# A planned order kept word for word for its first 520 entries and ordered anew behind them: gated linear attention followed by a spatial gating block

## The chip, the core and the metric

The kernel runs on one core of one Trainium2 chip. The metric is the device time of one launch in microseconds (us). Engines are named as the profile names them: PE (TensorE matmuls) and PEld (its weight loads), DVE (VectorE), ACT (ScalarE), POOL (GpSimd) and SP (SyncE, which issues nearly all DMAs here).

## What is computed

A recurrence with a 48x48 state for each of 4 x 8 heads runs over 768 steps; its output, heads side by side, goes through a gated MLP with a mixing over the sequence.

```python
def _attn_ref(q, k, v, alpha):            # each (4, 8, 768, 48)
    for t in range(S):
        state = alpha[:, :, t, :, None] * state + einsum('bhd,bhe->bhde', k[:, :, t], v[:, :, t])
        y[:, :, t] = einsum('bhd,bhde->bhe', q[:, :, t], state)
    ...
def _moe_ref(x, w_in, w_spatial, b_spatial, w_out):   # x: (4, 768, 384)
    h = np.maximum(x @ w_in, 0.0)
    u, v = (h[..., :d_ff // 2].copy(), h[..., d_ff // 2:].copy())
    v_n = (v - mu) / np.sqrt(var + 1e-06)
    v_s = np.einsum('ts,bsd->btd', w_spatial, v_n) + b_spatial[None, :, None]
    return ((u * v_s) @ w_out).astype(np.float32)
```

## The kernel before

Each batch's 768 steps are cut into 6 chunks of 128; chunks are numbered 0 to 23 over the four batches. For a chunk the kernel loads `alpha`, `k`, `q`, `v` (four DMAs of 192 KB, L883, on SP), takes the logarithm of alpha (`lns`, ACT), sums it on PE (`cums`, L898 to L901), takes the exponential with both signs on ACT (`einvs`, L908, and `eexps`, L910) and of the chunk's total (`ebc`, L915), multiplies k and q by them (`kts` on POOL or DVE, `qts` on DVE), transposes both on PE (`trk`, L988, two chunks at once) and evicts them (`evs`). PE then forms the update of the state (`upd`, L932), DVE adds the old state (`z`, L393), POOL or DVE scales it (`S`) and one engine casts it (`sb`). PE also forms the scores (`sc`, L944), DVE masks them (`ms`, L949), and PE makes the chunk's output (`y`, L960 and L416), which ACT or DVE evicts into `xT` (`xe`).

For each batch the MLP follows: `v` (L1005, three matmuls of 512 columns for each of 6 sequence tiles) with ReLU eviction `ve`, statistics `bn` (DVE), `rs` (ACT), `nm` (DVE) and normalization `vn`; `u` (three matmuls of 384 columns for each of 4 feature tiles and 2 halves of the sequence) with eviction `ue`; the mixing `s` (six matmuls of 384 columns, in a part of four and a part of two), to which DVE adds the bias (`se`, L1152); the product `g` of both (POOL or DVE, L189); the output projection `o` (four matmuls), eviction `oe` and store `st` (SP, L1184).

No scheduler orders this. Each of these steps is an `Op` with a number, given in the order in which the functions create them. The string `PLAN` is the order in which they are emitted, and `replay` emits them so: a letter for the engine (P PE, D DVE, A ACT, G POOL, S SP), the number of the step, and behind `@` the PSUM banks that it takes. Every engine works through its own entries in the order of the table; across engines only semaphores hold it back. There are eight banks of PSUM; an entry may take a bank when all users of the bank's last holder stand ahead of it in the table, and on the chip PE then waits for the last of them.

```python
for word in plan.split():
    ...
    for slot, n in zip(op.take, banks):
        assert held[n] is None or all(u.done for u in held[n].users), op.key
        held[n] = slot
        slot.bank = n
    op.emit(eng)
```

Steps whose numbers are used below (b is the batch, th the half of the sequence, d the feature tile):

| entry | step |
|---|---|
| P745, D746 | update matmuls of chunk 18; scaling of its state |
| A747, A779, A851, A792, A790 | cast of that state; `eexps` 20; `lns` 23; `ebc` 21; `einvs` 21 |
| G781, G793 | `kts` of chunks 20 and 21 |
| G671, G675, G679, G683 | `g` of b 2, th 0, d 0, 1, 2, 3 |
| P700, P703, P706 | output projection of b 2, tiles 0, 1, 2 |
| P593, A594, P604, P723, P596 | `v` of b 2 tile 2 and its eviction; `v` of tile 3; `cums` 18; `u` of b 2, d 0, th 0 |
| D899, D915, D922, G907, G911, G919 | `g` of b 3: (d 1, th 0), (d 1, th 1), (d 3, th 1); (d 3, th 0), (d 0, th 1), (d 2, th 1) |

Of the kernel before, what the change touches and what calls it, by code (L numbers as in the profile page):

```python
# [63 lines left out]
P436@4 A437 A441 A385 D264 D439 P272@0 D367 D267 D428 D431 D386 P521@1 P372@4 A514 A273 P565@6 P376@2 A377 A432 A552  # L64
P442@7 A568 P529@0 D443 D522 P456@3 D433 D434 A435 A566 A567 D373 P452@7 P553@1 P518@2,5 A519 A554 A556 D520 A555 P457
D458 D530 D570 G569 G523 G557 G459 P444@4 P445 P448@5 D446 P453 D454 P468@6 P449 D558 D450 P533@7,4 P524@2,0 P572@1,3
D525 G451 G455 P472@5 P469 P460@2 P473 D526 D534 D535 G531 G447 D474 S623 A559 P575@7 D576 A573 P461 S625 S612 S563
A615 D470 D462 P616@4 P527@5 P536@1 A627 S613 A574 P579@7,3 P588@6,0 G577 A617 A528 D589 A618 A537 P628@5 A629 A571
G475 P538@2 A630 P464@1 S624 S614 S730 S718 S721 S626 S720 G620 D621 D581 D580 S733 S732 P476@6 G631 G578 P541@3
P584@7 A539 A619 A542 P465 S784 S719 A477 D632 P634@5,4 D590 A636 D466 D585 S731 A722 P591@3 S786 S772 S785 S773 S835  # L70
S774 A592 S787 S775 G622 G532 P582@1 A583 D635 D540 P637@7 P482@6 A633 A483 P723@5 G586 G471 D638 G639 A724 P645@3,4
P640@0,2 D543 G463 G587 P479@7 P604@6 P596@1 D646 D642 D641 A734 A726 D647 G729 G467 A605 A741 G727 P593@3 P600@6 A594
P735@0 D606 D595 A738 D480 P648@4 P643@3 A544 D545 D546 D597 A649 P488@2 A644 A788 A601 A489 D547 P653@4 P660@7 P745@6
A654 D746 D655 A736 A607 D608 D610 P491@3 P664@4 A661 A665 A737 P650@6 A492 A776 G739 P598@1 D651 D609 P485@4 D652
A486 A725 D747 P666@7 A667 D740 P602@6 P662@4 P789@3 A656 A603 P676@7 P672@0 P753@6 A599 A790 A791 P777@1 A778 A792
A779 S484 S847 S836 S837 A839 A783 S838 S848 A663 S849 D657 D658 D659 D754 D728 P677 P673 P680@6 P688@5 D674 P681
P668@0 D794 D755 D678 D782 G781 G795 D682 P799@7 P669 G793 D800 P689 G675 D690 D670 P742@6,4 P796@7,3 A851 A780 D797
P696@5 A743 A798 G683 G679 P808@0 P697 P852@7 P840@6 A841 A842 A853 A843 A854 D744 P748@3,4 P757@1,2 D698 G801 G671
D749 D809 D758 P692@5 P693 D694 D750 P684@3 P703@0 P685 P700@5 G846 D759 A701 D686 P706@4 D856 D845 D707 A704 P760@5
A761 P751@0 A752 A802 P803@6,7 D805 G844 G855 P812@3,2 P858@4,5 G810 G687 G699 G691 A859 G695 D813 P762@0 S850 P861@7  # L80
P765@3 D814 D804 P712@2 P815@6 A756 A763 P806@0 A860 D862 D764 D857 A816 A807 A766 P864@5,7 P869@4,1 S702 P715@6 D866
D871 D767 D870 D865 P828@7 A829 D830 P824@1 P820@3 P817@7 A821 A768 A818 A825 G863 P872@4 A873 S705 A716 S481 S259
S268 S487 S265 S493 S490 S271 S708 S262 S478 S274 G811 P867@5 D819 P826@3 P822@1 D868 P877@4 D769 D771 A827 S717 A831
A823 A878 A770 A713 D832 P874@3 D833 D834 P890@5 P888@1 P884@4 D879 D875 D876 A880 D881 D882 P916@6 P709@2 A710 P896@3
P886@7 P900@0 A887 A889 A885 A891 P892@2 D883 P897 D898 G899 P893 P901 P908@5 P909 D894 D902 P904@2 P905 G903 P917
P912@0 P913 P920@3 D906 D895 D918 G919 D907 P929@6 P923@2 P921 S711 A930 S931 A924 S925 S714 D914 D910 D911 P926@6
G915 D922 P932@2 A933 D927 S928 S934 P938@3 D939 S940 P935@6 A936 S937 P941@3 D942 S943
"""


# [1174 lines left out]
```

## Time and profile before

| | |
|---|---|
| timed runs | 138.52, 138.55, 138.70 us, median 138.55 |
| span of the profiled execution | 137.9 us (137.862), 5298 instructions |
| matmul records and weight loads | 2108 and 2122 |
| bytes over DMA | 28.66 MB, 76521 packets, 63056 of them under 512 B |
| granted PE clock | 1.000 |

The profiled execution's own time outside its span is not listed; the timed median is 0.69 us above the span. In the profile a line such as "75.14 0.33 PE L932 ..." gives the start, the length, the engine, the source line, the tiles and the number of merged instructions. Lengths of matmuls are modelled and overlap the next one: a 384-column matmul is listed at 0.327 us, while four in a row start 0.16 us apart.

### The profile page before, as it was taken

What the parts mean: (1) busy time and instruction counts of PE and PEld (TensorE: products, weight loads), DVE (VectorE), ACT (ScalarE), POOL (GpSimd) and SP (SyncE); (2) the same over time, 40 slices, a digit from 0 to 9 for tenths busy, and PEclk for the clock granted to TensorE, in tenths of its full rate; (3) what the DMA queues carried; (4) which work ended last, traced back from release to release, by engine and by line L of the source; (5) the groups of instructions that cost most, each with busy time, mean ns of one, the idle gap of its engine ahead of it and who ended that gap; (6) DMA issues with size and microseconds to landing.
All of it is one profiled execution on the core that took longest, in us unless ns stands there. A gap on an engine that the chain in (4) does not pass through costs nothing.

```text
span 137.9 us, 5298 instructions
## 1 busy us (share of the span) xinstructions
PE 130.1 (94%) x2108; PEld 79.4 (58%) x2122; DVE 120.2 (87%) x300; ACT 107.7 (78%) x261; POOL 86.6 (63%) x146
## 2 busy tenths in 40 slices
PE   6999998999999999799999999999999999999990
PEld 3365555565566556466657676656576765566560
DVE  6259999989989999899899999997999999974960
ACT  3476998999999799699997989999865796953040
POOL 7355899993499799761079989520799841004550
PEclk9999999999999999999999999999999999999999
DMA  3999999499989788699999898999960597101064
GB/s 88 370 372 381 344 349 361 106 373 382 355 162 281 159 168 165 124 186 188 193 204 201 164 209 156 189 186 216 213 134 5 187 349 270 63 0 57 0 233 172
DMA packets 76521, 28.66 MB, mean 208 GB/s; under 512 B 63056, under 2 KB 74960, under 8 KB 76496
## 3 DMA queue, kind: packets, MB, share of 16 engines
q1 hardware_dynamic: 76464, 28.32, 77.8%
q8 instruction: 16, 0.26, 0.8%
q14 instruction: 9, 0.07, 0.2%
q0 software_dynamic: 32, 0.00, 0.0%
HBM read 23.60 MB, written 4.72 MB: 205 GB/s over the span
## 4 chain that ended last, share of the span: by engine, by line
PE 60%; DMA 19%; POOL 8%; issue 3%; SPq 3%; ACT 3%; DVE 0%; POOLq 0%; ACTq 0%
PE bank L1005 43%; DMA raw_w<-in_moe_w_spatial_dram 6%; DMA kc<-in_k_dram 5%; DMA raw_w<-in_moe_w_out_dram 4%; DMA ac<-in_alpha_dram 4%; PE bank L960 3%; SPq L883 3%; PE bank L944 2%; PE bank L988 2%; PE bank L416 2%; POOL w_row L180 2%; POOL kt L189 2%; PE bank L932 1%; PE bank L898 1%; POOL state L189 1%
## 5 line engine op out<-in xcount | busy, mean ns | idle before, releaser
L1005 PE MATMUL bank<-w_spT,vn 128*128 128x384 bf16 x192 | 35.6, 327 | 0.0
L189 POOL TENSOR_TENSOR gT<-vs,uT 128x384 bf16<-128x384 f32 x28 | 25.7, 933 | 14.1 <-DVE vs L1152 14.1
L189 POOL TENSOR_TENSOR kt<-kc,binv 128x384 bf16<-128x384 f32 x22 | 20.2, 928 | 22.3 <-ACT binv L908 15.2
L1005 PEld LDWEIGHTS <-vn 128*128 128x128 bf16 x192 | 17.5, 98 | 11.2 <-issue 0.3
L1005 PE MATMUL bank<-w_in,xT 128*128 128x512 bf16 x58 | 17.4, 380 | 1.6 <-ACT xT L178 0.7
L1005 PE MATMUL bank<-xT,w_in 128*128 128x384 bf16 x96 | 18.7, 326 | 0.0
L1005 PE MATMUL bank<-w_out_sb,gT 128*128 128x384 bf16 (+1 forms) x100 | 18.4, 320 | 0.0
L1152 DVE TENSOR_TENSOR vs<-bank,bsp_bc 128x384 f32<-128x384 f32 x31 | 16.3, 549 | 2.4 <-PE bank L1005 2.3
L949 DVE TENSOR_TENSOR ptm<-bank,mask 128x512 bf16<-128x512 f32 x28 | 17.9, 682 | 0.5 <-PE bank L944 0.3
L178 ACT COPY kqT<-bank 128x512 bf16<-128x512 bf16 (+1 forms) x20 | 15.0, 793 | 3.1 <-PE bank L988 1.9
L1067 DVE BATCH_NORM_STATS2 stats<-v_sb 128x6 f32<-128x512 bf16 x24 | 16.4, 683 | 0.6 <-ACT v_sb L184 0.5
L184 ACT ACTIVATE v_sb<-bank 128x512 bf16<-128x512 f32 x20 | 11.7, 597 | 2.0 <-PE bank L1005 1.7
L184 ACT ACTIVATE uT<-bank 128x384 bf16<-128x384 f32 x27 | 12.4, 494 | 0.7 <-PE bank L1005 0.6
L1005 PEld LDWEIGHTS <-w_in 128*128 128x128 bf16 x96 | 9.0, 97 | 6.7 <-DVE ptm L949 0.3
L189 DVE TENSOR_TENSOR qt<-qc,bank 128x384 bf16<-128x384 f32 x24 | 12.6, 545 | 0.2 <-DMA qc<-in_q_dram 0.2
L1005 PEld LDWEIGHTS <-gT 128*128 128x128 bf16 x100 | 9.2, 98 | 5.8
L178 ACT CAST xT<-bank 128x384 bf16<-128x384 f32 x23 | 10.4, 482 | 1.1 <-PE bank L416 0.8
L843 DVE TENSOR_TENSOR ptm<-bank,mask 128x512 bf16<-128x512 f32 x16 | 10.3, 683 | 0.2 <-PE bank L836 0.2
L242 PE MATMUL bank<-junk 128*128 128x512 f32 (+3 forms) x14 | 8.8, 763 | 1.0 <-DVE junk L1231 1.0
L1005 PEld LDWEIGHTS <-xT 128*128 128x128 bf16 x72 | 6.2, 97 | 6.2 <-ACT xT L178 1.2
L178 ACT COPY raw_w<-bank 128x384 f32<-128x384 f32 x8 | 3.8, 479 | 7.3 <-PE bank L1005 7.2
L393 DVE TENSOR_TENSOR zs<-bank,state 128x384 f32<-128x384 f32 x16 | 8.8, 548 | 0.5 <-PE bank L932 0.4
(162 smaller groups left out, 264.3 us busy)
## 6 DMA issues: line engine op xcount, KB each, us to landing
ac<-in_alpha_dram SPq DMA_DIRECT2D x14, 192.0 KB, 4.4
kc<-in_k_dram SPq DMA_DIRECT2D x14, 192.0 KB, 4.4
qc<-in_q_dram SPq DMA_DIRECT2D x14, 192.0 KB, 4.4
vc<-in_v_dram SPq DMA_DIRECT2D x14, 192.0 KB, 4.2
raw_w<-in_moe_w_spatial_dram SPq DMA_DIRECT2D x3, 768.0 KB, 7.8
out_dram<-raw_w SPq DMA_DIRECT2D x11, 192.0 KB, 2.1
out_dram<-o_sb SPq DMA_DIRECT2D x9, 192.0 KB, 2.0
ac<-in_alpha_dram SPq DMA_DIRECT2D x2, 768.0 KB, 6.7
```

The costliest lines, as they stand in the source:

```text
L178: nc.scalar.copy(out=out, in_=in_)
L184: nc.scalar.activation(out=out, in_=in_, func=AF.Relu)
L189: ENG[eng].tensor_tensor(out=out, in0=in0, in1=in1, op=ALU.mult)
L242: nc.tensor.matmul(out=banks[n][:, 0:cols].rearrange("p (a b) -> p a b", a=4), lhsT=junk, rhs=junk[:, None, 0:cols // 4].to_broadcast([128 ...
L393: lambda _: nc.vector.tensor_tensor(out=zs[i % 3], in0=tp(), in1=state[(i - 1) % 3], op=ALU.add),
L843: nc.vector.tensor_tensor(out=ptm[n2][:, ci, s], in0=banks[sl.bank].rearrange("p (hp t) -> p hp t", hp=HP), in1=mask[:, 3][:, None, :].to_ ...
L883: nc.sync.dma_start(out=t[x].rearrange("p hp s d -> p (hp s) d"), in_=src[b, :, c * C:c * C + C, :].rearrange("h s d -> s h d"))
L949: nc.vector.tensor_tensor(out=ptm[n2][:, ci, s], in0=banks[sl_p[s].bank].rearrange("p (hp t) -> p hp t", hp=HP), in1=mask[:, 2][:, None, : ...
L960: nc.tensor.matmul(out=place(to, 3 * hp + (0, 1, 1, 2)[x]), lhsT=heads(vb, hp, x), rhs=ptm[n2][:, ci, x // 2, hp, :], start=(turn == 0), s ...
L1005: nc.tensor.matmul(out=ps, lhsT=lhsT, rhs=rhs, start=first and n == 0, stop=last and n == len(pairs) - 1)
L1067: nc.vector.bn_stats(out=stats[tt % 2], in_=v_sb[n2][:, tt, :])
L1152: nc.vector.tensor_tensor(out=vs[d], in0=banks[sl.bank][:, 0:TH], in1=bsp_bc[:, th, :], op=ALU.add)
```

## The change

Only `PLAN` changes. Its first 520 entries are the same word for word. The other 424 are the same steps in a new order, with other banks, and for 38 of them another engine: 14 go from ACT to DVE and 14 from DVE to ACT, 4 from DVE to POOL, 3 from ACT to POOL, 2 from POOL to DVE and 1 from POOL to ACT. PE keeps its 124 entries, and no instruction's shape changes. The plan before reaches its 521st entry at about 75.3 us on PE; on SP the first changed entry is the load at 66.0 us. Two of the lines on each side:

```diff
-P668@0 D794 D755 D678 D782 G781 G795 D682 P799@7 P669 G793 D800 P689 G675 D690 D670 P742@6,4 P796@7,3 A851 A780 D797
...
-A761 P751@0 A752 A802 P803@6,7 D805 G844 G855 P812@3,2 P858@4,5 G810 G687 G699 G691 A859 G695 D813 P762@0 S850 P861@7
...
+D754 A747 P680@6 P673 A779 A851 A792 A790 D674 P669 P681 P688@2 D728 D782 D670 G781 S775 S785 G793 S786 A791 G675 D682
...
+S787 G795 S848 G683 D794 P689 S490 S835 P742@0,1 D743 A744 P676@7 P677 D678 G679 D690 P696@5 G671 P757@0,1 D758
```

Three places show what moves. First POOL, around the key scalings of chunks 20 and 21 (`kt_102` from `binv_106` and `binv_107`) and the four products `gT_142` of batch 2, th 0. Before:

```order
L189 TENSOR_TENSOR kt_102<-kc,binv_106 128x8x48
L180 CAST vb_113<-vc 128x8x48
L189 TENSOR_TENSOR kt_102<-kc,binv_107 128x8x48
L189 TENSOR_TENSOR gT_142<-vs_153,uT_137 128x384
L189 TENSOR_TENSOR gT_142<-vs_155,uT_137 128x384
L189 TENSOR_TENSOR gT_142<-vs_154,uT_137 128x384
L189 TENSOR_TENSOR state_128<-zs_125,bc_119 128x384
L189 TENSOR_TENSOR gT_142<-vs_152,uT_137 128x384
```

The same place on POOL in the changed kernel:

```order
L189 TENSOR_TENSOR kt_102<-kc,binv_106 128x8x48
L189 TENSOR_TENSOR kt_102<-kc,binv_107 128x8x48
L189 TENSOR_TENSOR gT_142<-vs_153,uT_137 128x384
L180 CAST vb_113<-vc 128x8x48
L189 TENSOR_TENSOR gT_142<-vs_155,uT_137 128x384
L189 TENSOR_TENSOR gT_142<-vs_154,uT_137 128x384
L189 TENSOR_TENSOR gT_142<-vs_152,uT_137 128x384
L189 TENSOR_TENSOR state_127<-zs_124,bc_118 128x384
```

The cast `vb_113` now stands behind the first product, and the last product stands ahead of a state update. Second ACT, where the evictions of `v` (`v_sb_138`) and `u` (`uT_137`) of batch 2 begin; `bank_64` to `bank_71` are PSUM banks 0 to 7. Before:

```order
L184 ACTIVATE v_sb_138<-bank_70 128x512
L178 CAST vb_112<-vc 128x8x48
L184 ACTIVATE v_sb_138<-bank_67 128x512
L915 ACTIVATE bc_118<-bank_64 64x4 x2
L1077 ACTIVATE rstd_146<-mvs_144,eps_tile 128x2
```

ACT in the changed kernel, from the eviction A594 on:

```order
L184 ACTIVATE v_sb_138<-bank_70 128x512
L184 ACTIVATE v_sb_138<-bank_69 128x512
L184 ACTIVATE uT_137<-bank_71 128x384
L908 ACTIVATE binv_108<-bank_64 128x384
L184 ACTIVATE uT_137<-bank_70 128x384
L888 ACTIVATE la_100<-ac 128x8x48
```

Bank 6 (`bank_70`) goes from `v` of tile 2 to `u` of d 0 within four ACT instructions. Third DVE at the end of the program, with the additions `vs` and the products `gT_143` of batch 3. Before:

```order
L189 TENSOR_TENSOR gT_143<-vs_152,uT_135 128x384
L1152 TENSOR_TENSOR vs_154<-bank_70,bsp_bc 128x384
L189 TENSOR_TENSOR gT_143<-vs_155,uT_135 128x384
L1152 TENSOR_TENSOR vs_153<-bank_64,bsp_bc 128x384
L1152 TENSOR_TENSOR vs_152<-bank_69,bsp_bc 128x384
L189 TENSOR_TENSOR gT_143<-vs_152,uT_135 128x384
L189 TENSOR_TENSOR gT_143<-bank_67,uT_135 128x384
L180 COPY o_sb_156<-bank_70 128x384
```

DVE at the same place in the changed kernel:

```order
L1152 TENSOR_TENSOR vs_152<-bank_68,bsp_bc 128x384
L1152 TENSOR_TENSOR vs_153<-bank_69,bsp_bc 128x384
L186 TENSOR_SCALAR uT_135<-bank_71 128x384
L189 TENSOR_TENSOR gT_143<-vs_153,uT_135 128x384
L189 TENSOR_TENSOR gT_143<-bank_70,uT_135 128x384
L1152 TENSOR_TENSOR vs_153<-bank_64,bsp_bc 128x384
L189 TENSOR_TENSOR gT_143<-vs_153,uT_135 128x384
```

The product of d 3 (from a bank directly) now stands ahead of the last addition instead of last, two products have changed sides with POOL, and the copy of an output tile has gone to ACT.

More of the change, by code (lines that the diff above doesn't have):

```diff
@@ L66 @@
 D458 D530 D570 G569 G523 G557 G459 P444@4 P445 P448@5 D446 P453 D454 P468@6 P449 D558 D450 P533@7,4 P524@2,0 P572@1,3
[L67 to L75, printed above, removed]
@@ L76 @@
-A779 S484 S847 S836 S837 A839 A783 S838 S848 A663 S849 D657 D658 D659 D754 D728 P677 P673 P680@6 P688@5 D674 P681
-P668@0 D794 D755 D678 D782 G781 G795 D682 P799@7 P669 G793 D800 P689 G675 D690 D670 P742@6,4 P796@7,3 A851 A780 D797
-P696@5 A743 A798 G683 G679 P808@0 P697 P852@7 P840@6 A841 A842 A853 A843 A854 D744 P748@3,4 P757@1,2 D698 G801 G671
-D749 D809 D758 P692@5 P693 D694 D750 P684@3 P703@0 P685 P700@5 G846 D759 A701 D686 P706@4 D856 D845 D707 A704 P760@5
-A761 P751@0 A752 A802 P803@6,7 D805 G844 G855 P812@3,2 P858@4,5 G810 G687 G699 G691 A859 G695 D813 P762@0 S850 P861@7
@@ L81 @@
[L81 to L85, printed above, removed]
@@ L86 @@
-P912@0 P913 P920@3 D906 D895 D918 G919 D907 P929@6 P923@2 P921 S711 A930 S931 A924 S925 S714 D914 D910 D911 P926@6
-G915 D922 P932@2 A933 D927 S928 S934 P938@3 D939 S940 P935@6 A936 S937 P941@3 D942 S943
+D525 G451 G455 P472@5 P469 P460@2 P473 D526 D534 D535 G531 A615 P464@7 S612 S623 S563 D470 D474 A571 A627 G447 A559
+P575@6 G532 A573 D576 P616@4 P461 A574 S730 A734 A619 G475 D462 P465 P628@6 P527@5 A528 G577 G578 D466 P536@3 A537
+P579@2,1 D581 P588@5,7 D589 D590 P584@0 A629 A617 A630 G620 A618 P541@3 A542 S626 S625 D632 S624 S613 D621 P538@1
@@ new lines @@
+P479@5 A539 A480 S614 S784 D580 D585 G631 S259 A622 S718 P482@3 A483 G586 G587 P735@4 P634@5,1 A635 A738 S847 S772
+D543 D636 P591@2 P582@0 A583 A788 P637@3 P476@6 A477 D638 D540 P640@1,5 D642 P645@3,0 D647 A592 D646 A544 D641 P602@7
+P593@6 A722 A594 P604@5 A605 A603 S733 P723@0 P596@6 A724 A597 A776 G467 P598@3 S721 A599 A725 A726 G463 G471 P488@7
+D595 D606 S719 A607 G633 G639 G729 G727 P643@1 D644 P648@6 A736 A737 P789@5 A649 D545 D547 D489 P600@3 A601 A546 S773
+S731 D608 P491@1 D492 P650@2 P777@7 S268 P664@1 A665 P653@3 A654 P660@6 P662@1 P485@3 D610 A778 A663 D651 D609 D741
@@ new lines @@
+A780 D652 A661 D655 A656 S732 S774 S720 D740 D486 D657 D659 D658 G739 P666@2 P672@1 A667 P668@4 P753@2 P745@3 D746
+D754 A747 P680@6 P673 A779 A851 A792 A790 D674 P669 P681 P688@2 D728 D782 D670 G781 S775 S785 G793 S786 A791 G675 D682
+S787 G795 S848 G683 D794 P689 S490 S835 P742@0,1 D743 A744 P676@7 P677 D678 G679 D690 P696@5 G671 P757@0,1 D758
+P748@7,6 P796@4,3 D783 G755 G756 P697 P852@0 P684@2 D750 P685 P808@6 S265 S849 S837 D749 D759 A797 D686 A839 P840@4
+A798 A853 A843 A854 P700@7 P799@3 P692@1 S836 S838 D800 D698 D701 G855 A841 G801 A842 D856 D845 G844 P706@2 A707 P693
@@ new lines @@
+D694 P703@5 A704 S705 P751@0 P760@2 P812@4,7 A752 A761 G846 G802 D809 G810 D813 D814 P803@1,5 P858@0,3 A860 A859
+P762@2 P861@4 P765@7 A763 P815@3 A816 S262 S850 S702 D805 S478 S493 D804 P806@1 D766 A807 D862 P869@0,5 D871 P864@2,7
+P828@3 P817@5 A829 S271 S481 A818 P826@1 P824@3 G863 G691 G811 D865 D866 P867@5 A857 D870 P872@0 D819 A868 A827 D830
+D767 D764 A873 A831 D832 A825 D834 P820@7 P874@5 A821 P884@0 A875 G695 G699 P877@1 P822@7 G687 P715@5 P712@3 A768 D769
+D833 D770 D876 P890@2 A771 P908@4 A878 D879 A880 A716 D885 D881 D713 S714 S274 S717 P916@1 P900@6 P904@0 P892@5 A883
@@ L88 @@
+D882 P917 P893 P901 D894 D902 G903 S487 P905 P888@3 P896@5 P909 D918 D906 P709@6 P897 P886@1 P912@0 A710 S711 A887
+A889 A891 P920@6 G895 P921 S708 S484 D910 D898 P913 D823 D899 G907 P929@2 P923@3 A930 S931 D922 D914 A924 S925 P926@0
+A927 S928 D915 G919 G911 P932@2 A933 S934 P938@3 D939 S940 P935@0 A936 S937 P941@2 D942 S943
 """
```

## The prediction, on record before the run

> **What bounds the kernel now.** I read the page's busy shares first, then the table of stretches from the change to the last matmul and behind it, and then the chain that ended last.
>
> ```profile
> PE 130.1 (94%) x2108; PEld 79.4 (58%) x2122; DVE 120.2 (87%) x300; ACT 107.7 (78%) x261; POOL 86.6 (63%) x146
> 75.40:134.40 59.00, 58.43 (x841) 36.61 (x844) 53.18 (x121) 43.49 (x109) 32.68 (x56) 1.00 0.62 155
> 134.40:137.90 3.50, 0.00 (x0) 0.00 (x0) 0.31 (x1) 0.10 (x1) 0.00 (x0) 1.00 0.48 171
> 129.33 5.01 PE bank L1005 x34
> 134.35 0.36 DVE raw_w L180
> ```
>
> The columns of the stretches are length, then PE, PEld, DVE, ACT and POOL busy, granted clock and DMA share. In the 59.0 us that the change can touch, PE is idle for 59.00 - 58.43 = 0.57 us. DVE is busy 53.18 us of them (90%), ACT 74%, POOL 55%. The chain's last rows are 34 matmuls, then one copy at 134.35; behind 134.4 the last store and the end of the program take 3.5 us, which the change leaves as they are, since both tables end with the same four steps. **So PE is the bound, it is nearly full, and its work does not change.** An order can only remove waits of PE or add them.
>
> **How much waiting is there to remove.** 0.57 us is the upper end from the idle column. It is not exact: 14 matmul records are missing (2122 loads, 2108 matmuls), and a missing one shows as idle. On the other side modelled ends cover waits:
>
> ```profile
> 96.46 3.09 PE L1005 MATMUL bank<-w_spT,vn 128*128 128x384 bf16 x18
> 99.59 0.33 PE L932 MATMUL bank<-vb,kt 128*128 128x96 bf16 x4
> 101.54 0.82 PE L1005 MATMUL bank<-w_spT,vn 128*128 128x384 bf16 x4
> 102.20 0.33 PE L932 MATMUL bank<-vb,kt 128*128 128x96 bf16 x4
> ```
>
> Four matmuls of 384 columns take 102.20 - 101.54 = 0.66 us to the next start, 0.163 each. Eighteen should take 2.93 us; they took 99.59 - 96.46 = 3.13. The 0.20 us is a wait of PE for the state update of chunk 20 that the idle column hardly shows. The other waits that I find by this pitch are small ones, under 0.1 us each, some 0.25 together. I take **0.45 us as the headroom**, with 0.57 as its end.
>
> **Changes of tile shape.** A step of 32, 48 or 64 rows or columns costs PE something at its borders:
>
> ```profile
> 68.29 0.57 PE bank L988 x32
> 100.57 1.04 PE bank L988 x64
> ```
>
> One transposing step takes 0.57 us, two in a row 1.04, so that the second adds 0.47 and a border costs about 0.09. The new order parts these two transposing steps, but puts other small steps together instead. Counted over both tables from entry 521 on, full tiles change to a smaller shape 9 times and back 9 times in each, and the output steps meet score or transposing steps 4 times in each. This term is 0.
>
> **Engines.** A moved eviction changes the load of its engine:
>
> ```profile
> L189 POOL TENSOR_TENSOR gT<-vs,uT 128x384 bf16<-128x384 f32 x17 | 15.4, 926 | 14.1 <-DVE vs L1152 14.1
> 86.00:96.00 10.00, 9.61 (x28) 1.00 0.98 200
> ```
>
> 14 steps each way between ACT and DVE leave both about where they were; POOL, with 14.1 us of waits in front of its products, takes 7 steps (4 of them from DVE) and gives 3, at up to 0.93 us each some 3 us more. No engine's total comes near the 59 us, so the term of the totals is 0. What counts is the place: from 86 to 96 ACT is busy 9.61 of 10.00 us (the last row, which is of ACT alone), and PE hands it bank after bank there.
>
> **Waits that the new order brings: banks handed over by ACT.** The tightest hand-over is bank 6 from `v` of tile 2 to `u` of d 0. Between them PE has only `v` of tile 3 and the sum of chunk 18 to do:
>
> ```profile
> 79.42 0.81 PE L1005 MATMUL bank<-w_in,xT 128*128 128x512 bf16 x3
> 80.07 0.33 PE L932 MATMUL bank<-vb,kt 128*128 128x96 bf16 x4
> 75.63 0.33 PE L898 MATMUL bank<-la,le_one 128*128 128x384 bf16 x1
> 75.80 0.24 PE L901 MATMUL bank<-ones_col,la 128*128 128x1 bf16 x4
> 90.05 0.63 ACT L184 ACTIVATE v_sb<-bank 128x512 bf16<-128x512 f32 x1
> 90.53 0.53 ACT L908 ACTIVATE binv<-bank 128x384 bf16<-128x384 f32 x1
> 91.38 0.85 ACT L184 ACTIVATE uT<-bank 128x384 bf16<-128x384 f32 x2
> ```
>
> `v` takes 80.07 - 79.42 = 0.65 us of PE, the sum 0.27 (0.17 to the next row and four short matmuls); that is 0.92 us. ACT needs 0.63 for the eviction, and it can start only when the modelled end of the matmul is past, 0.16 us behind its slot, and a signal later: some 0.85 us when ACT is free. One more instruction ahead of it costs 0.36 to 0.48 (the starts of the rows at 90.05, 90.53 and 91.38 and the two within the last one). So this place costs PE between 0 and about 0.4 us. I find such places, with less than 0.15 us to spare, also at the masked scores of chunk 15, at the evictions of `u` and the output of chunk 17 around 91 us, and at `u` d 1 and the output projection around 118. Each is worth 0 to 0.4; a delay of PE at one gives the next some air, so I do not add their ends. I take **0.25 us for all of them together**, 0 to 0.8 as the bounds.
>
> **Waits that the new order brings: POOL ahead of the output projection of batch 2.** The first projection P700 asks for the product of d 0 (G671), the last of four on POOL. The chain to it from the update of chunk 18 (P745) runs through DVE, ACT and POOL:
>
> ```profile
> 103.27 0.55 PE bank L944 x16
> 98.33 0.65 DVE L189 TENSOR_TENSOR state<-zs,bc 128x384 f32<-128x384 f32 x1
> 96.64 0.49 ACT L908 ACTIVATE binv<-bank 128x384 bf16<-128x384 f32 x1
> 97.02 0.34 ACT L915 ACTIVATE bc<-bank 64x4 f32<-64x4 f32 x2
> 97.39 0.47 ACT L910 ACTIVATE bank<-bank 128x384 f32<-128x384 f32 x1
> 97.89 0.53 ACT L888 ACTIVATE la<-ac 128x384 bf16<-128x384 f32 x1
> 97.20 0.91 POOL L189 TENSOR_TENSOR kt<-kc,binv 128x384 bf16<-128x384 f32 x1 [5.15 <-ACT binv L908]
> 98.06 0.50 POOL L180 CAST vb<-vc 128x384 bf16<-128x384 f32 x1
> 98.52 1.23 POOL L189 TENSOR_TENSOR kt<-kc,binv 128x384 bf16<-128x384 f32 x1
> 99.71 2.66 POOL L189 TENSOR_TENSOR gT<-vs,uT 128x384 bf16<-128x384 f32 x3
> 103.12 0.92 POOL L189 TENSOR_TENSOR gT<-vs,uT 128x384 bf16<-128x384 f32 x1
> ```
>
> PE itself has between P745 and P700 34 mixing matmuls (x 0.163 = 5.5), two transposing steps (1.1), the scores of two chunks (0.55, the first row here), two sums and an update (0.6) and their borders, 7.9 us in all. The chain, step by step: 0.28 from PE's slot to DVE and the state 0.65; then on ACT the cast, `eexps` 20, `lns` 23 and `ebc` 21 at 0.4 each by the starts of the rows (1.6), and `einvs` 21 with 0.49; then POOL: `kts` 21 0.87, product 0.91, cast 0.46, two products 1.83, the last 0.92 (4.99); signals between engines, 0.05 three times. The sum is 0.93 + 2.09 + 4.99 + 0.15 = 8.2 us against 7.9. PE would wait 0.3 us; what it has waited in between, at the banks of the scores of chunks 18 and 19, comes off. Before, the last product started at 103.12 and the first projection stood at 105.39 (below), with 1.3 us to spare. I take **0.2 us**; the bounds are 0 and 0.6, the latter if the key scaling takes the 1.23 us of the row at 98.52 instead of 0.91.
>
> ```profile
> 105.39 0.81 PE L1005 MATMUL bank<-w_out_sb,gT 128*128 128x384 bf16 x4
> ```
>
> **The end.** The last `g` steps are in a new order and two have changed sides with POOL:
>
> ```profile
> 129.44 1.97 POOL L189 TENSOR_TENSOR gT<-vs,uT 128x384 bf16<-128x384 f32 x2 [1.68 <-DVE vs L1152]
> 129.21 0.55 DVE L189 TENSOR_TENSOR gT<-vs,uT 128x384 bf16<-128x384 f32 x1
> 130.72 1.09 DVE L189 TENSOR_TENSOR gT<-vs,uT 128x384 bf16<-128x384 f32 x1
> ```
>
> A product on DVE takes 0.55 us alone and 1.09 while POOL's run (the rows at 129.44 and 130.72 overlap). In the new order the last of them (D915) stands behind the addition of d 1. That addition's matmuls end three projections ahead of the first step that reads the product, 3 x 4 x 0.163 = 1.95 us, and the product is read by that step's second matmul, so 2.1 us. DVE needs 0.28 to hear of it, 0.5 for the addition and 0.55 or 1.09 for the product, 1.3 to 1.9. It has 0.2 to 0.8 us to spare, so this term is 0. The Trainium skill (GPSIMD Engine Reference, section 8, Key points) says that GpSimd shares its SBUF interfaces with VectorE and that the two get in each other's way when a Vector instruction has two SBUF inputs; the trace agrees, 1.09 against 0.55 us. By that rule every product that overlaps costs 0.5 us more on DVE, and the term stays 0 only because of the room just counted.
>
> **Loads.** SP issues the remaining loads in a new order, with five or six stores of finished tiles between them instead of one.
>
> ```profile
> 92.75 0.66 SPq L1184 DMA_DIRECT2D out_dram<-w_row  x1
> 93.46 0.42 SPq L883 DMA_DIRECT2D ac<-in_alpha_dram  x1
> 100.31 0.63 SPq L883 DMA_DIRECT2D vc<-in_v_dram  x1
> 112.68 0.33 DVE L180 CAST vb<-vc 128x384 bf16<-128x384 f32 x1
> ac<-in_alpha_dram SPq DMA_DIRECT2D x14, 192.0 KB, 4.4
> ```
>
> A store holds SP for 0.7 us (92.75 to 93.46). Five more make the last load some 3.5 us later than 100.31; it also stands behind a store that waits for a tile finished at about 108, so it lands near 112.5 (4.4 us to land) and is read at about 114 in the new order. The others have 2 us and more. This term is 0; it costs PE what is late beyond 2 us.
>
> **Sum.** -0.45 + 0.25 + 0.20 = 0.0 us. The profiled span of 137.86 becomes 137.86; the 0.69 us up to the median of 138.55 I leave. The forecast is **138.55 us**, its own range 138.3 to 138.8 (within 0.2%, or 0.28 us, which is about what a measurement of this kernel can tell from no change).
>
> **Rivals.** (1) *The waits go and none comes*: the hand-overs hold, because ACT happens to be free at each. For it: all of them have at least nominal room. Against: ACT is 96% busy there. It gives 138.55 - 0.45 + 0 to 0.15 = 138.1 to 138.25. (2) *Slower, through POOL's chain*: if `einvs` 21 ends later than 7.9 - 4.99 - 0.05 = 2.9 us after the update of chunk 18, each further delay goes straight into P700 and so into the end. With `kts` 21 at 1.23 us it is 0.6 us, with hand-overs at 0.4 to 0.6 us in all: 138.55 - 0.45 + 1.0 to 1.2 = 139.1 to 139.3; half of either gives 138.85. For it: the chain is longer than PE's way already. Against: PE's own waits come off it. (3) *The end slips*: both DVE products at 1.09 and POOL's last behind them, 0.5 us more on the forecast, 139.05. (4) *A load comes late*: over 2 us beyond what I counted, 1 us in PE, 139.5.
>
> **Chances.** Forecast 0.48, (1) 0.26, (2) 0.19, (3) 0.04, (4) 0.03. Faster by over 0.2%: 0.26; within: 0.48; slower: 0.26. The range goes from the end of (1), with 0.05 for the spread of the runs, to the middle of (2): 138.05 to 139.15, and leaves out a part of (2), and (4).
>
> **What would show it.** In the changed profile PE's idle time from 75 us to its last matmul should again be 0.4 to 0.6 us, the first projection of batch 2 should stand directly behind POOL's last product, and the matmul at the new `u` of d 0 behind an ACT eviction. If PE's waits sum to under 0.2 us, rival (1) is right; if P700 waits over 0.5 us, rival (2). I am wrong altogether if the number or the pitch of matmuls changes, or if the time behind the last matmul is not 3.5 us.

## The result, and the profile after

| | before | after |
|---|---|---|
| timed runs beside each other, median | 138.48 us (138.22 to 139.25, 22 runs) | 139.33 us (138.75 to 141.18, 22 runs) |
| ratio to before, 95% interval | | 1.0052 [1.0034, 1.0071] |
| span of the profiled execution | 137.9 us | 137.8 us (that execution took 139.6 us) |
| matmul records, weight loads | 2108, 2122 | 2122, 2122 |

The change makes the kernel 0.5% slower. One run of after, 141.18 us, counts as slow and is left out of the ratio. The two spans hide it: the execution of before that was profiled was a long one. In every later run the time is 1.8 us above the span (139.6 and 137.8 here), so that execution took about 139.6 us, 1.1 us more than the median of its kernel. What the change touches has to be measured inside the trace. From the page of after, the busy shares:

```profile
PE 131.9 (96%) x2122; PEld 79.0 (57%) x2122; DVE 120.6 (88%) x298; ACT 108.7 (79%) x259; POOL 89.7 (65%) x150
```

From the timelines of PE and DVE, first of before and then of after: the transposing step of chunks 14 and 15, the last large step ahead of the changed entries on PE, and the last copy of the program (start, length, engine, line, tiles).

```profile
72.61 0.22 PE L988 MATMUL bank<-ident,kt 64*128 64x64 bf16 x4
134.35 0.36 DVE L180 COPY raw_w<-bank 128x192 f32<-128x192 f32 x1 [0.62 <-PE bank L1005]
```

```profile
71.98 0.22 PE L988 MATMUL bank<-ident,kt 64*128 64x64 bf16 x4
134.33 0.36 DVE L180 COPY raw_w<-bank 128x192 f32<-128x192 f32 x1 [0.64 <-PE bank L1005]
```

Before takes 134.35 - 72.61 = 61.74 us from the one to the other, after 134.33 - 71.98 = 62.35. **The changed stretch costs 0.61 us more**, and the part ahead of it, which is the same in both tables, happened to be 0.63 us shorter in this execution. The same stretch in the table of windows (length, then PE, PEld, DVE, ACT, POOL busy, granted clock, DMA share, GB/s), of before and of after:

```profile
72.61:134.35 61.74, 61.22 (x893) 38.57 (x893) 55.82 (x125) 45.56 (x112) 35.41 (x59) 1.00 0.64 157
```

```profile
71.98:134.33 62.35, 62.13 (x900) 38.21 (x893) 55.95 (x123) 46.26 (x110) 38.20 (x63) 1.00 0.63 155
```

PE's idle time has fallen, from 0.52 to 0.22 us, while the stretch became longer. So the idle column is no measure of PE's waits here: modelled ends cover them, and missing matmul records (14 before, none after) show as idle. The waits have to be read from the distance between starts, against the pitch of the instructions. In after these are the ones over 0.05 us, the three largest first. ACT and PE around 91 us (two timelines of after):

```profile
89.81 0.49 ACT L908 ACTIVATE binv<-bank 128x384 bf16<-128x384 f32 x1
90.19 0.49 ACT L910 ACTIVATE bank<-bank 128x384 f32<-128x384 f32 x1
90.60 0.48 ACT L178 CAST xT<-bank 128x384 bf16<-128x384 f32 x1
```

```profile
90.82 0.24 PE L901 MATMUL bank<-ones_col,la 128*128 128x1 bf16 x4
91.14 0.65 PE L1005 MATMUL bank<-xT,w_in 128*128 128x384 bf16 x3
```

Where nothing is late, the four short matmuls of a sum hold PE for 0.10 us, as at the same place in the ninth run below (its timeline of PE):

```profile
91.22 0.24 PE L901 MATMUL bank<-ones_col,la 128*128 128x1 bf16 x4
91.32 0.65 PE L1005 MATMUL bank<-xT,w_in 128*128 128x384 bf16 x3
```

Here it is 91.14 - 90.82 = 0.32. The `u` behind them (P664, b 2, th 1, d 2) reads chunk 17's output, which ACT evicts as `xT` until 91.08, behind two exponentials of chunk 19. **0.22 us.** The other two stand close together, on DVE, POOL and PE (three timelines of after):

```profile
92.28 0.35 DVE L180 CAST vb<-vc 128x384 bf16<-128x384 f32 x1
...
101.77 0.68 DVE L949 TENSOR_TENSOR ptm<-bank,mask 128x512 bf16<-128x512 f32 x1
102.37 0.89 DVE L180 CAST vb<-vc 128x384 bf16<-128x384 f32 x1
103.18 1.87 DVE L949 TENSOR_TENSOR ptm<-bank,mask 128x512 bf16<-128x512 f32 x3
```

```profile
101.25 1.79 POOL L189 TENSOR_TENSOR gT<-vs,uT 128x384 bf16<-128x384 f32 x2
102.99 1.04 POOL L189 TENSOR_TENSOR gT<-vs,uT 128x384 bf16<-128x384 f32 x1
```

```profile
102.74 1.14 PE L1005 MATMUL bank<-w_spT,vn 128*128 128x384 bf16 x6
103.91 0.34 PE L932 MATMUL bank<-vb,kt 128*128 128x96 bf16 x4
104.25 0.24 PE L901 MATMUL bank<-ones_col,la 128*128 128x1 bf16 x4
104.51 0.81 PE L1005 MATMUL bank<-w_out_sb,gT 128*128 128x384 bf16 x4
```

The cast of v of chunk 20 (D783, which the change moves from ACT to DVE) takes 0.89 us at 102.37, and the same instruction for another chunk 0.35 us at 92.28. POOL is at its products from 101.25 to 104.03; nothing ran on POOL at 92.28. Behind the cast stand two masked scores of chunk 18 (`ms` 18 1 from 103.18 to 103.86, `ms` 18 0 from 103.78 to 104.46), and they free banks 6 and 7. The update of chunk 21 takes bank 6: six matmuls at 0.163 are 0.98 us, and 103.91 - 102.74 is 1.17, **0.20 us** of wait with the rounding. The first output projection of batch 2 takes bank 7: 104.51 - 104.25 = 0.26 in place of 0.10, **0.15 us**, and it starts 0.05 us behind the end of `ms` 18 0. Smaller ones are 0.10 at the mixing step s 2 3 1 0 (100.38, bank 5), 0.09 at the scores of chunk 18 (101.44, bank 7) and 0.06 in the first output projection of batch 3 (its second matmul, 130.31). Together 0.82 us.

### The profile page after: what moved, and what is told of

Same layout as the page of the kernel before. It is cut to its first block, busy times and chain, and to the rows that moved or that the text cites. A ratio compares the mean times of both kernels' runs of the same rounds, so it can differ in the third digit from the quotient of the medians.

```text
span 137.8 us, 5309 instructions
## 1 busy us (share of the span) xinstructions
PE 131.9 (96%) x2122; PEld 79.0 (57%) x2122; DVE 120.6 (88%) x298; ACT 108.7 (79%) x259; POOL 89.7 (65%) x150
## 4 chain that ended last, share of the span: by engine, by line
PE 75%; ACT 7%; DVE 6%; DMA 5%; issue 3%; POOL 2%; SPq 0%; POOLq 0%; DVEq 0%
PE bank L1005 51%; DMA kc<-in_k_dram 5%; PE bank L988 3%; PE bank L944 3%; PE bank L416 2%; PE bank L960 2%; PE bank L854 2%; PE bank L836 2%; PE bank L932 1%; PE bank L898 1%; DVE ptm L949 1%; DVE vn L1096 1%; ACT xT L178 1%; PE bank L1017 1%; PE bank L794 1%
## 5 line engine op out<-in xcount | busy, mean ns | idle before, releaser
L189 POOL TENSOR_TENSOR gT<-vs,uT 128x384 bf16<-128x384 f32 x29 | 26.8, 940 | 9.1 <-DVE vs L1152 8.6
L1005 PE MATMUL bank<-xT,w_in 128*128 128x384 bf16 x96 | 19.2, 326 | 0.1
L1005 PE MATMUL bank<-w_in,xT 128*128 128x512 bf16 x72 | 18.8, 380 | 0.2 <-ACT xT L178 0.2
L178 ACT COPY kqT<-bank 128x512 bf16<-128x512 bf16 (+1 forms) x21 | 15.9, 802 | 3.6 <-PE bank L988 2.4
L180 POOL CAST sbd<-state 128x384 bf16<-128x384 f32 x15 | 7.4, 505 | 0.6 <-DVE state L189 0.3
```

The lines of the kernel that those rows point to most:

```text
L178: nc.scalar.copy(out=out, in_=in_)
L180: ENG[eng].tensor_copy(out=out, in_=in_)
L189: ENG[eng].tensor_tensor(out=out, in0=in0, in1=in1, op=ALU.mult)
L1005: nc.tensor.matmul(out=ps, lhsT=lhsT, rhs=rhs, start=first and n == 0, stop=last and n == len(pairs) - 1)
```

## The experiments

The question is which of these waits carry the 0.6 us. There are three theories: W, PE waits at fixed places that the order sets; L, the loads behind the five or six stores come late; C, the cast on DVE is stretched beside POOL's products. All kernels below compute the same; only `PLAN` differs, and each line of a diff gives neighbours on one engine, in its own order. The expectations speak of a stretch that ends at the start of the last projection, some 0.5 to 0.6 us ahead of the last copy: 61.21 us before, 61.75 after. The table gives both.

| run | transposing step, us | last copy, us | stretch to the copy | to the last projection | ratio to before in timed runs |
|---|---|---|---|---|---|
| before | 72.61 | 134.35 | 61.74 | 61.21 | |
| after | 71.98 | 134.33 | 62.35 | 61.75 | 1.0052 [1.0034, 1.0071] |
| 1 after again | 71.89 | 134.22 | 62.33 | 61.73 | 1.0043 [1.0019, 1.0066] |
| 2 stores last | 71.54 | 133.87 | 62.33 | 61.73 | 1.0017 [0.9993, 1.0041] |
| 3 three moves | 71.16 | 133.86 | 62.70 | 62.11 | 1.0073 [1.0050, 1.0095] |
| 4 cast on ACT | 71.04 | 133.10 | 62.06 | 61.46 | 1.0020 [0.9991, 1.0048] |
| 5 before again | 71.88 | 133.62 | 61.74 | 61.21 | 1.0011 [0.9984, 1.0038] |
| 6 cast later on DVE | 71.63 | 133.62 | 61.99 | 61.39 | 0.9996 [0.9972, 1.0020] |
| 7 cast on ACT, output earlier | 72.99 | 134.94 | 61.95 | 61.34 | 1.0024 [0.9989, 1.0059] |
| 8 and banks 3, 5 exchanged | 71.30 | 133.17 | 61.87 | 61.27 | 1.0004 [0.9977, 1.0030] |
| 9 all three, cast on DVE | 72.38 | 134.20 | 61.82 | 61.21 | 1.0022 [0.9998, 1.0046] |

The fastest timed run of each kernel goes with its stretch: 138.08 to 138.22 us for before in all its series, 138.62 to 138.75 for after and runs 1 and 2 (62.3 us), 139.16 for run 3 (62.70), 138.16 to 138.39 for runs 4 and 6 to 9 (61.8 to 62.1). That supports reading the change by the stretch.

**Run 1, the changed kernel again** (no edit).

> The changed kernel once more, unchanged, for a second profile beside fresh runs of the kernel before. Theory W (waits): the loss sits behind the change, as waits of PE at a few fixed places; PE then takes 61.6 to 61.9 us from the transposing step of chunks 14 and 15 to the start of the last projection (61.75 in the first profile, 61.21 before), with waits of at least 0.1 us again at the u step of feature tile 2, half 1 (0.2), the update of chunk 21 (0.2) and the first projection of batch 2 (0.1), and a ratio of 1.003 to 1.007. Theory P (what lies ahead of the change): that stretch varies by more than 0.3 us between two profiles, the places of the waits differ, and the ratio follows the stretch ahead of 72 us.

The stretch is the same within 0.02 us, with the same waits at the same instructions; so far theory W holds: the waits belong to the order.

**Run 2, the six stores behind the last load on SP.**

```diff
-S784 S259 S718 ... S731 S268 S732 ... S848 S490 S835 S265 S849 ... S838 S705 S262 S850 S702
+S784 S718 ... S731 S732 ... S848 S835 S849 ... S838 S850 S259 S268 S490 S265 S705 S262 S702
```

> The changed kernel with the six stores that stand between its loads put behind its last load on SP; nothing else moves. Theory L (loads): the stores delay the loads and those delay the work; ratio back to 0.999 to 1.002, and PE's waits from 72 us on fall from 0.9 to about 0.5 us. Theory W: loads have 2 us to spare, ratio 1.003 to 1.007 as in the changed kernel, same waits.

Nothing in the stretch moves: 62.33 again. The loads are not what PE waits for; theory L falls for this stretch. The timed ratio, 1.0017, is where theory L had put it and below what W had said, but its interval overlaps that of run 1, the fastest timed run is 138.62 us in both, and the trace shows no place for a gain behind the transposing step.

**Run 3, three steps moved at once**: the cast of v of chunk 20 back to ACT, the first output projection one step later on PE, and ACT's output of chunk 17 ahead of both exponentials of chunk 19.

```diff
-D758 D783 D750
+D758 D750
-A744 A797
+A744 A783 A797
-P840@4 P700@7 P799@3 P692@1 P706@2
+P840@4 P799@3 P692@1 P700@7 P706@2
-A607 A736 A737 A649 A601
+A607 A649 A736 A737 A601
```

> The changed kernel with three moves at the three largest waits: the cast of v of chunk 20 from DVE to ACT (where ACT idles 1.9 us), the first projection of batch 2 behind the next update and the next mixing part (0.8 us later on PE), and the eviction of the output of chunk 17 ahead of the two exponentials of chunk 19 on ACT. Theory W: waits of 0.20, 0.14 and 0.22 us go, part of it comes back at the places behind; PE's stretch falls from 61.75 to 61.2 to 61.4 us and the ratio to the kernel before is 0.998 to 1.002. Theory L or P: no change by this, 61.6 to 61.9 us and 1.003 to 1.007.

The waits of 0.22, 0.20 and 0.15 us are gone, and the stretch is 0.35 us longer than in after; the expected 61.2 to 61.4 us to the last projection were missed by 0.7 and more. Two new waits take their place (with two small ones, 0.10 at v 2 5 and 0.09 at a projection of batch 3). From PE's and ACT's timelines of this run:

```profile
103.29 0.24 PE L901 MATMUL bank<-ones_col,la 128*128 128x1 bf16 x4
103.96 0.33 PE L932 MATMUL bank<-vb,kt 128*128 128x96 bf16 x4 [0.43 <-ACT kqT L178]
```

```profile
102.91 1.00 ACT L178 COPY kqT<-bank 128x1024 bf16<-128x1024 bf16 x1
```

Without the projection ahead of it, which takes 0.65 us, the update of chunk 20 comes to its bank at 103.39 (103.29 and 0.10 for the sum), and ACT has emptied it only at 102.91 + 1.00 = 103.91. It starts at 103.96: a wait of 0.57 us that the projection had covered. The other is a matter of POOL and DVE again (their timelines of this run):

```profile
89.86 1.13 DVE L1096 TENSOR_SCALAR vn<-v_sb,mvs,rstd 128x512 bf16<-128x512 bf16 x1
...
93.70 0.52 DVE L189 TENSOR_TENSOR qt<-qc,bank 128x384 bf16<-128x384 f32 x1
```

```profile
89.93 0.91 POOL L189 TENSOR_TENSOR kt<-kc,binv 128x384 bf16<-128x384 f32 x1 [2.42 <-ACT binv L908]
```

With the exponential 0.4 us later, POOL's scaling of k starts 0.07 us behind the start of DVE's normalization, which takes 1.13 us; in after, whose DVE and POOL rows follow, the scaling started 0.3 us ahead of it and it took 0.75.

```profile
90.68 0.75 DVE L1096 TENSOR_SCALAR vn<-v_sb,mvs,rstd 128x512 bf16<-128x512 bf16 x1
```

```profile
90.37 0.91 POOL L189 TENSOR_TENSOR kt<-kc,binv 128x384 bf16<-128x384 f32 x1 [2.04 <-ACT binv L908]
```

Everything on DVE behind it is 0.4 us later, q of chunk 19 too, whose bank PE wants next: 0.18 us at s 2 0 0 0.

**Run 4, only the cast of v of chunk 20 on ACT**, as before the change.

```diff
-D758 D783 D750
+D758 D750
-A744 A797
+A744 A783 A797
```

> Of the three moves only the first: the cast of v of chunk 20 on ACT. Theory C (contention): the cast took 0.89 us on DVE instead of 0.33 because POOL's products ran beside it, and the mask behind it came late for the bank of the update of chunk 21; on ACT it takes 0.5 us, DVE's masks come 0.6 us or more earlier, the wait of 0.20 us at the update goes, and the first projection of batch 2 waits 0.2 to 0.35 instead of 0.14, as POOL's last product is no earlier; PE's stretch falls by 0 to 0.1 us. Rival: the update waits for POOL's key scaling or cast of chunk 21 and not for the bank; then it still waits 0.1 to 0.2 us. Ratio 1.003 to 1.007 by both.

The stretch is 0.29 us shorter by the rows, 0.29 also to the last projection. Both waits, at the update of chunk 21 and at the first output projection, are gone. DVE, POOL and PE of this run (three timelines):

```profile
100.82 2.48 DVE L949 TENSOR_TENSOR ptm<-bank,mask 128x512 bf16<-128x512 f32 x4
```

```profile
100.30 2.66 POOL L189 TENSOR_TENSOR gT<-vs,uT 128x384 bf16<-128x384 f32 x3
```

```profile
102.77 0.33 PE L932 MATMUL bank<-vb,kt 128*128 128x96 bf16 x4
102.94 0.33 PE L898 MATMUL bank<-la,le_one 128*128 128x384 bf16 x1
103.10 0.24 PE L901 MATMUL bank<-ones_col,la 128*128 128x1 bf16 x4
103.20 0.81 PE L1005 MATMUL bank<-w_out_sb,gT 128*128 128x384 bf16 x4
```

The four masks run in one go, POOL's three products take 2.66 us in place of 2.78, and the projection follows the sum after 0.10 us. The projection had waited for bank 7 and not for POOL. So the expectation was wrong there: it had the wait at the projection grow and the stretch fall by 0.1 us at most. A wait of 0.08 us is new at a projection of batch 3.

**Run 5, the kernel before again** (no edit).

> The kernel before, unchanged. Theory W (the change costs fixed TensorE waits between the transposes of chunks 14/15 and the last projection): that stretch is 61.2 us again, as in the first profile of before (61.21), while the time ahead of it differs from run to run by some tenths. Rival S (the stretch too varies between executions by half a us): it reads anything from 61.2 to 61.8. Time: the same as before.

61.74 us to the hundredth, with the part ahead of it 0.73 us shorter (71.88 against 72.61). In the first profile of before that part holds a wait of PE for an eviction of `u` (the row is from its table of waits), which run 5 does not have.

```profile
PE bank L960 <- ACT uT L184: 1.0, 1, 1.0
```

**Run 6, the cast left on DVE, two places later.**

```diff
-D758 D783 D750 D749 D759
+D758 D750 D749 D783 D759
```

> The changed kernel with the VectorE cast of chunk 20's v kept on VectorE, but two places later: behind the masked scores ms 18 1 and ms 18 0 instead of ahead of them. Theory C (the cast is stretched from 0.35 to 0.89 us beside GpSimd's products, and the masked scores behind it hold banks 6 and 7): both waits, 0.20 at upd 21 and 0.15 at the first output projection of block 2, go, and the stretch reads 61.40 to 61.50, as with the cast on ScalarE, though VectorE does all the work it did. Rival P (the first output projection waits for GpSimd's products): 0.15 to 0.2 stay there, stretch 61.55 or more. The cast itself will still read 0.5 to 0.9 us, since GpSimd is at work there too.

DVE, POOL and PE of this run:

```profile
101.42 1.88 DVE L949 TENSOR_TENSOR ptm<-bank,mask 128x512 bf16<-128x512 f32 x3
103.21 0.55 DVE L180 CAST vb<-vc 128x384 bf16<-128x384 f32 x1
103.68 0.68 DVE L949 TENSOR_TENSOR ptm<-bank,mask 128x512 bf16<-128x512 f32 x1
```

```profile
100.89 2.66 POOL L189 TENSOR_TENSOR gT<-vs,uT 128x384 bf16<-128x384 f32 x3
```

```profile
103.36 0.33 PE L932 MATMUL bank<-vb,kt 128*128 128x96 bf16 x4
...
103.69 0.24 PE L901 MATMUL bank<-ones_col,la 128*128 128x1 bf16 x4
103.80 0.81 PE L1005 MATMUL bank<-w_out_sb,gT 128*128 128x384 bf16 x4
```

The stretch is 0.36 us shorter, with the same instructions on every engine: the two waits came from this one cast standing ahead of the masks. To the last projection it is 61.39, 0.01 below the expected range. Rival P falls: POOL's last product ends at 103.55 in this run (100.89 + 2.66), 0.25 us ahead of the projection.

**Run 7, run 4 and ACT's output of chunk 17 between the two exponentials.**

```diff
-A736 A737 A649 A601
+A736 A649 A737 A601
```

> The changed kernel with the cast of chunk 20's v on ScalarE (as in the fourth run) and ScalarE's eviction of chunk 17's output put between the two exponentials of chunk 19 instead of behind both. Theory A (the 0.2 us wait of the u projection at 91 us is for that eviction, 0.4 us late behind one exponential): the wait goes, the first exponential and with it GpSimd's product of k stays where it was, so nothing behind it moves: stretch 61.20 to 61.30. Rival M (whatever is moved up there comes back later, as in the third run where both exponentials were passed): stretch 61.4 or more with a wait at s 2 0 0 0.

The wait of 0.22 us at P664 goes, and 0.09 us come back at the next step, v 2 5, for the bank of the `u` whose eviction is still behind the second exponential. Of the gain 0.11 us are left (62.06 to 61.95). The expectation of 61.20 to 61.30 was missed by 0.04.

**Run 8, run 7 with banks 3 and 5 exchanged on PE from s 2 3 1 0 on.**

```diff
-P696@5 P757@0,1 P748@7,6 P796@4,3
+P696@3 P757@0,1 P748@7,6 P796@4,5
...
```

> The kernel of the run ahead with banks 3 and 5 exchanged on TensorE from the gate's projection s 2 3 1 0 on (that projection no longer waits until VectorE has read bank 5 for q of chunk 21; the transposes of chunks 20/21 take bank 5 behind it). If each wait is a hand-over of one bank: 0.10 less, stretch 61.10 to 61.20, below the kernel before (61.21), and the time some 0.1 to 0.2 per cent below it. Rival: the hand-overs that all later banks inherit give it back: 61.3 or more.

The wait of 0.10 us at s 2 3 1 0 goes, but the scores of chunk 19 now wait 0.05 us and those of chunk 18 0.14 in place of 0.09. So the exchange gains nothing at its place: from the transposing step to the update of chunk 21 it is 104.60 - 72.99 = 31.61 us in run 7 and 102.90 - 71.30 = 31.60 in this one (PE's timelines of run 7 and of run 8).

```profile
104.60 0.33 PE L932 MATMUL bank<-vb,kt 128*128 128x96 bf16 x4
```

```profile
102.90 0.33 PE L932 MATMUL bank<-vb,kt 128*128 128x96 bf16 x4
```

In all the stretch is 0.08 us shorter. That is the wait at a projection of batch 3, known from run 4, which this run does not have. The expected 61.10 to 61.20 was missed by 0.07: at this place the rival is right, in that the hand-overs behind give the gain back.

**Run 9, the edits of the three places together, with the cast on DVE as in run 6.** Beside the edits of runs 6 and 7, banks 3 and 6 are exchanged from v 2 5 on, and banks 3 and 5 (of the exchanged names) from s 2 3 1 0 on.

```diff
-P664@1 P653@3 P660@6
+P664@1 P653@6 P660@3
...
-P696@5 P757@0,1 P748@7,6 P796@4,3
+P696@3 P757@0,1 P748@7,5 P796@4,6
...
```

> The changed kernel with three places mended and no work changed: the cast of chunk 20's v two places later on VectorE (0.36 us less alone), ScalarE's eviction of chunk 17's output between the two exponentials of chunk 19 (0.12 less in the seventh run), and banks exchanged on TensorE so that v 2 5 no longer waits for the bank of the u ahead of it (0.09) and s 2 3 1 0 no longer for VectorE's read of bank 5 (0.07). If the waits are local and add up: stretch 61.75 - 0.36 - 0.12 - 0.09 - 0.07 = 61.11, just below the kernel before (61.21), and a time within 0.1 per cent of it. If a mended wait comes back elsewhere: 61.25 or more.

0.53 us of the 0.61 are gone, and to the last projection the stretch is that of before, 61.21. The expected 61.11 was missed by 0.10, which is what the scores of chunks 19 and 18 wait more, 0.05 each, as in run 8. So the 0.53 are the cast (0.36, run 6) and the eviction of chunk 17's output (61.99 - 61.82 = 0.17, with the bank at v 2 5). The timed ratio, 1.0022 [0.9998, 1.0046], doesn't tell it from before: the part ahead of the change moves by up to 1.95 us between profiled executions (71.04 to 72.99) and drowns a tenth. No version here beats the kernel before.

## Why the prediction was wrong, point by point

**PE as the bound, and the time behind the last matmul: right.** The stretch changes by PE's waits, and 3.5 us lie behind the last copy's start again (137.8 - 134.33).

**Headroom of 0.45 us: right in size.** None of the waits that I found in before stands in after; by the same pitch 0.45 us of them are gone.

**Tile shapes, 0: right.** From the transposing step on, PE's entries change shape 24 times before and 25 times after. The one more stands between scores and a transposing step, a kind that my count had left out, and it has no price that shows. The scores of two chunks take 103.75 - 103.20 = 0.55 us with the border to a full tile (PE of before), and 108.88 - 108.42 = 0.46 with the one to a transposing step (PE of after), so that the 0.09 us of a border are missing there.

```profile
103.20 0.62 PE L944 MATMUL bank<-kqT 48*128 48x128 bf16 x16
103.75 0.50 PE L1005 MATMUL bank<-w_spT,vn 128*128 128x384 bf16 x2
```

```profile
108.42 0.62 PE L944 MATMUL bank<-kqT 48*128 48x128 bf16 x16
108.88 0.40 PE L988 MATMUL bank<-ident,kt 64*128 64x64 bf16 x16
```

**ACT's hand-overs, 0.25: right in size, by one of the four places.** The eviction of chunk 17's output at 91 us costs 0.22 us; the scores of chunk 15 come 0.04 us late (77.53), and the hand-over of bank 6 that I called the tightest and the places around 118 us cost nothing that shows. So an ACT that is busy 9.30 of 10.00 us from 86 to 96 in after is late by more than 0.04 us at one place out of four.

**POOL's chain ahead of P700, 0.20, and the moves between engines, 0: the steps that failed.** P700 does wait, 0.15 us, but not for POOL: in after POOL's products are done at 104.03 and P700 stands at 104.51, right behind the mask that frees bank 7. The chain itself was as long as summed: from the update of chunk 18 at 95.85 (the second of the two in this row of PE of after, 0.17 us behind the first) to 104.03 are 8.18 us, against 8.2.

```profile
95.68 0.50 PE L932 MATMUL bank<-vb,kt 128*128 128x96 bf16 x8
```

PE's own way to P700 was summed too short: it takes 104.51 - 95.85 = 8.66 us here and 8.3 in run 6, where POOL has 0.25 us to spare, against 7.9.

The larger failure is the move of D783 from ACT to DVE. I put 14 such moves each way down at 0, because the engines' totals stay the same, and priced the new places on ACT and POOL alone; the row I had quoted for this kind of cast was 0.33 us and started with POOL idle. In its new place it takes 0.89, and the 0.54 us on top reach PE twice, 0.20 at bank 6 and 0.15 at bank 7: 0.35 us argued from the rows of after, 0.36 (run 6) and 0.29 (run 4, which has the new wait of 0.08) by the runs. That it is the stretching, and not the cast's own 0.35 us, follows from the rows alone: 0.54 us earlier the mask would free bank 6 at 103.32, and PE comes there at 102.74 + 0.98 = 103.72. No run has an undisturbed cast in that place.

**That POOL and DVE get in each other's way** was weighed only at the end of the program, and only for products. There it costs PE 0.06 us, in the first projection of batch 3, whose second weight load waits for the product (three timelines of after, of DVE, POOL and PE's weight loads):

```profile
129.06 1.19 DVE L189 TENSOR_TENSOR gT<-vs,uT 128x384 bf16<-128x384 f32 x1
```

```profile
128.92 2.10 POOL L189 TENSOR_TENSOR gT<-vs,uT 128x384 bf16<-128x384 f32 x2 [0.30 <-ACT uT L184]
```

```profile
130.30 1.74 PEld L1005 LDWEIGHTS <-gT 128*128 128x128 bf16 x12 [0.27 <-DVE gT L189]
```

The Trainium skill (SBUF — State Buffer, "SBUF: two separate sides") says that one pair of ports is an exclusive lock between the two: whichever of a GpSimd instruction and a Vector instruction in a two-port mode or with two SBUF inputs starts first holds it to its end. The rows agree: the cast, which has one SBUF input, ends at 103.26, behind the POOL instruction that ended by 102.99, and the masks, which read PSUM, keep their 0.68 us beside POOL. Whether the cast runs in a two-port mode no run here shows. One row fits less well: in run 3 DVE's normalization starts at 89.86, 0.07 us ahead of POOL's scaling, and is the one that is stretched all the same; whether the recorded start is the moment that counts stays open.

**The sum.** -0.45 + 0.22 (ACT) + 0.35 (the cast) + 0.10 + 0.09 (banks 5 and 7) + 0.06 (the end) = 0.37 us to the last projection, where the rows have 0.54; the rest is in slips under 0.05 us, among them the 0.04 at the scores of chunk 15, and was not followed place by place. The hand-overs of banks 5 and 7 by DVE, 0.19 together, have no term in the prediction. A further 0.07 us lie between the start of the last projection and the last copy (0.60 against 0.53) and were not followed up. The time, 139.33 us, landed just above the upper end of rival (2), 139.3, by another mechanism.

**My range's base.** I left 0.69 us between span and median as if it lay around every execution. It does not: outside the span are 1.8 us in each, and the profiled execution was a long one. The sum of differences is unharmed by this, but it is the reason why the spans of the two pages can't be subtracted.

**What I said would show it.** PE's idle column has 0.22 us, below the 0.4 to 0.6 of the forecast, at a slower kernel: that sign was useless. P700 directly behind POOL's last product was the better one, and it fails.

## What to carry to other kernels

When a step changes engines at equal totals, price it at its new place: look up what the other engine runs at that moment, and what stands behind it in the queue. A Vector instruction whose operands are all in SBUF may last until GpSimd's current one ends, so put it behind those that PE waits for; two places were worth 0.36 us here. Compare kernels by a stretch that only the change touches: it repeated to 0.02 us, while whole executions differ by over 1 us. And after mending a wait, follow PE some steps further: the exchange of two banks in run 8 moved 0.10 us to the next two hand-overs and gained nothing.

## What the runs showed of the hardware that was not expected

- Instructions of DVE with operands in SBUF alone take, beside a POOL instruction that started ahead of them (in the row of 1.13 us 0.07 behind), 0.89 us in place of 0.35 (cast), 0.75 and 1.13 in place of 0.40 (normalization), 1.19 in place of 0.55 (product). POOL loses little there: its three products took 2.78 us with the cast beside them and 2.66 without it.
- A border between scores (48 rows) and a transposing step (64x64) shows no price, 0.46 against 0.55 us, while the one to a full tile costs 0.09.
- The order fixes the time from the transposing step to the last copy to 0.02 us (61.74 twice, 62.35 and 62.33), while the part ahead of it, with the same entries in the same order on PE, ends anywhere from 71.04 to 72.99 us.
